# A ring of exponentials with 21 instead of 14 tiles, and a smaller reserve for GpSimd's DMA descriptors

## The chip, the cores and the metric

The kernel runs on one core of a Trainium2 chip. The engines of the core work side by side, each through its own list of instructions in order: TensorE (PE in the profile; its weight loads are shown as PEld), VectorE (DVE), ScalarE (ACT), GpSimd (POOL) and SyncE (SP), whose queue issues the DMAs. They wait for each other through semaphores. The metric is device time in microseconds (us) from one execution of the program; several runs are made and the median is given.

## The reference

One transformer block on 2048 rows of 512 numbers: layer norm, attention with 32 query heads of width 16 that share one key and one value head, and a gate from a dense Mish layer.

```python
def _A_ref(x, wq, wk, wv, wo):
    B, S, D = x.shape
    H = 32
    Dh = D // H
    q = (lambda x, *d: x.transpose(*d))((x @ wq).reshape(B, S, H, Dh), 0, 2, 1, 3)
    k = x @ wk
    v = x @ wv
    scores = jnp.einsum("bhqd,bkd->bhqk", q, k) * (Dh ** -0.5)
    p = _softmax(scores, axis=-1)
    o = jnp.einsum("bhqk,bkd->bhqd", p, v)
    return (lambda x, *d: x.transpose(*d))(o, 0, 2, 1, 3).reshape(B, S, H * Dh) @ wo
...
x = A_x
xn = _layernorm(x, axis=-1)
s = _A_ref(xn, A_wq, A_wk, A_wv, A_wo)
g = _silu(_B_ref(xn, B_w1, B_b1, B_w2))
return x + s * g
```

`_B_ref` is a dense layer 512 to 1792, Mish, and a dense layer back to 512. Everything is float32.

## The kernel before, in words

The queries are cut into 4 chunks of 512 rows, and each chunk's 32 heads into 8 groups of 4 heads. That gives 32 groups `v`, and each group runs over the 16 blocks of 128 keys: 512 **steps** `s`. After a start of some 85 us, in which x is loaded, normalised and transposed and keys and values are made, a loop over the steps writes out the order of every engine by hand. In one step stand:

- four score matmuls `e` (line 908, function `e_one`): 128 keys against 512 queries of one head. A head takes 64 of TensorE's 128 rows, so two matmuls on different halves of the rows run at once. Their results go to a pool of three PSUM banks (`ps_e`), in turn. The fourth score of a step therefore takes the bank that the first one of the same step had, after ScalarE has read it.
- four exponentials `pt` on ScalarE (line 910), one for each score, 128 x 512, written to SBUF tiles of 2 KiB a partition with the tag `pt`. These tiles are **the ring**: `NPT` of them, used in turn. The step's exponentials are named `pt{s}_0` to `pt{s}_3`.
- about four matmuls `m` (line 928, `m_one`), scores of a later group, whose row maxima VectorE takes (`mb`, line 932). The maxima go back into the query tiles `qt` through DMAs, so that the exponential gets shifted scores.
- four to nine matmuls `xps` (line 112) of the projections and of the dense layers, as two half matmuls each. The function `waves` deals these, `e` and `m` out to the two halves of the rows. Between the two halves of a projection chunk it adds a wait by hand ("other half of the bank"): the first matmul of the second half waits for an operation of the step before, in most steps the third exponential.
- at the step's end four matmuls `pv` (line 982; eight rows in the profile), which multiply the exponentials of an earlier step by the values. `pv_to(s - 2)` puts them two steps behind, so a tile is read by the end of the third step after it was written. In the last 20 steps the order is another: there are no `m`, up to six scores stand in a row, and `pv` of several steps are done together.

Beside the four exponentials ScalarE has at most one or two other operations a step (Mish and the normalisation, as exponentials and logarithms: lines 671 to 763 and 1006 to 1010).

A tile that is used again brings waits with it. The exponential that writes a ring slot must wait until `pv` has read the slot's old content, and until the old exponential has written it; the first is a wait on PE's semaphore, which the exponential has anyway for its score, and the second is one on ScalarE's own semaphore (`Activation`). Where other waits make sure of it already, the wait is left out when the program is built. An instruction holds one wait; for a second one, a separate wait instruction is put ahead of it in the engine's list (EVENT_SEMAPHORE in the trace).

At the start the ring's tiles also take the 16 blocks of x (`load_x`):

```python
tag, n = ("pt", NPT) if 4 * c + tt < NPT else (("y0", "sc")[tt % 2], 1)
...
pt = sb.tile([P, C], F32, tag="pt", name=f"pt{s}_{i}", bufs=NPT)
r = act.activation(pt, e, AF.Exp, scale=0.25)
```

The first line above is line 215, the last two are 909 and 910. All DMAs are issued from SyncE's queue. The program also holds a reserve in SBUF for the descriptors of DMAs that GpSimd would issue, 16 KiB a partition at address 0 unless asked for otherwise.

Of the kernel before, what the change touches and what calls it, by code (L numbers as in the profile page):

```python
# [42 lines left out]
HOLD = 1  # L43
STEP_US = 2.95
XMAX = 8
NPT = 14
EM = "MEMEMEME"
MLAG = 4
NHB = 4
# [69 lines left out]
def block_kernel(ctx: ExitStack, tc: tile.TileContext, x, wq, wk, wv, wo, w1, b1, w2, out):  # L119
# [93 lines left out]
    def load_x(c):  # L213
        for tt in range(4):
            tag, n = ("pt", NPT) if 4 * c + tt < NPT else (("y0", "sc")[tt % 2], 1)
            xin[c, tt] = sb.tile([P, D], F32, tag=tag, name=f"xin{c}_{tt}", bufs=n)
# [680 lines left out]
    def e_one(s, i):  # L897
# [10 lines left out]
        pe.matmul(e, ks[o:o + 64, P * k:P * (k + 1)], q[o:o + 64, p], start=True, stop=True)  # L908
        pt = sb.tile([P, C], F32, tag="pt", name=f"pt{s}_{i}", bufs=NPT)
        r = act.activation(pt, e, AF.Exp, scale=0.25)  # L910
# [487 lines left out]

# [10 lines left out]
```

## Time and profile before

| | us |
|---|---|
| median of 3 runs | 1607.55 |
| lowest, highest | 1606.56, 1608.75 |
| span of the profiled execution | 1607.2 |
| TensorE busy | 1590.6 |
| VectorE busy | 1344.9 |
| ScalarE busy | 1298.3 |
| GpSimd busy | 625.4 |

The profile is of one execution. Of it the span is given, from the first to the last instruction; no other time of its own is listed. A line such as L910 names the line of the kernel that issued an instruction. "Busy" means that an instruction of the engine was under way; a matmul that waits inside the engine counts as busy. In lists of waits the row "ACT pt L910 <- PE e L908: 240.9, 455, 1.4" reads: ScalarE's exponentials sat idle until a score matmul for 240.9 us in total, 455 times, 1.4 us at the longest. Timeline rows are start, length, engine, line, operation, output <- inputs, count of merged instructions, and in brackets the idle time before and what ended it. Engine names with a q (ACTq) are what the engine's instruction queue does by itself.

### The profile page before, as it was taken

How to read it: one execution, taken by the hardware profiler on the slowest of the kernel's cores; microseconds unless marked ns; L12 is line 12 of the kernel's file. 1: busy time of each engine (PE TensorE's matmuls, PEld its weight loads, DVE VectorE, ACT ScalarE, POOL GpSimd, SP SyncE). 2: the span in 40 equal slices, each digit the busy share in tenths (PEclk: the TensorE clock that was granted, in tenths of full speed). 3: DMA queues.
4: the chain of work that ended last, by engine and by line, in shares of the span. 5: the costliest groups of instructions: out<-in, count | busy, mean ns of one | idle time of the engine just before them, and what ended most of it. 6: DMA issues, size and time to landing. Idle time of an engine off the chain costs nothing.

```text
span 1607.2 us, 31497 instructions
## 1 busy us (share of the span) xinstructions
PE 1590.6 (99%) x11611; PEld 847.8 (53%) x11611; DVE 1344.9 (84%) x2299; ACT 1298.3 (81%) x2512; POOL 625.4 (39%) x640
## 2 busy tenths in 40 slices
PE   9999999999999999999999999999999999999998
PEld 5445555555555555555555555555555555555544
DVE  8898888888888888888898988888888888888812
ACT  7478788688898778978988787787798878779885
POOL 3276278066355103612514322172152323315522
PEclk9899999999999999999999999999999999999999
DMA  6233133142321304212103231221331223022020
GB/s 192 72 116 96 51 108 115 29 149 83 101 90 38 111 16 140 64 48 88 39 24 109 64 116 44 87 71 35 96 109 58 83 61 97 24 96 70 8 86 27
DMA packets 73001, 125.08 MB, mean 78 GB/s; under 512 B 21520, under 2 KB 33808, under 8 KB 72848
## 3 DMA queue, kind: packets, MB, share of 16 engines
q1 hardware_dynamic: 72848, 123.08, 24.4%
q8 instruction: 92, 1.51, 0.4%
q14 instruction: 61, 0.50, 0.1%
HBM read 75.57 MB, written 26.21 MB: 63 GB/s over the span
## 4 chain that ended last, share of the span: by engine, by line
PE 96%; DVE 1%; ACT 1%; POOL 0%; DMA 0%; SPq 0%; issue 0%; DVEq 0%; POOLq 0%
PE xps L112 43%; PE pv L982 32%; PE e L908 9%; PE m L928 8%; PE xps L108 3%; PE kp L312 1%; DVE mb L932 1%; PE wop L108 1%; ACT pt L910 0%; PE xp L280 0%; DMA xin<-in_dram 0%; DVE xt L156 0%; SPq L217 0%; ACT hb L671 0%; PE ol L1045 0%
## 5 line engine op out<-in xcount | busy, mean ns | idle before, releaser
L932 DVE TENSOR_REDUCE mb<-m 128x1 f32<-128x512 f32 x2048 | 1271.2, 682 | 184.2 <-PE m L928 149.0
L910 ACT ACTIVATE pt<-e 128x512 f32<-128x512 f32 x2048 | 1068.2, 605 | 250.9 <-PE e L908 240.9
L928 PE MATMUL m<-ks,qt 48*128 48x512 f32 (+1 forms) x2048 | 845.8, 424 | 4.2 <-DVE mb L932 2.9
L908 PE MATMUL e<-qt,ks 64*128 64x512 f32 x2048 | 746.7, 408 | 2.4 <-ACT pt L910 1.6
L982 PE MATMUL pv<-pt,vaug 128*32 128x512 f32 x4096 | 543.1, 604 | 0.0
L928 PEld LDWEIGHTS m<-ks,qt 48*128 48x128 f32 (+1 forms) x2048 | 373.1, 186 | 76.3 <-DVE mb L932 38.0
L908 PEld LDWEIGHTS e<-qt,ks 64*128 64x128 f32 x2048 | 372.4, 186 | 26.2 <-ACT pt L910 11.1
L112 PE MATMUL xps<-xt,ws 64*128 64x512 f32 x1266 | 351.2, 409 | 0.9 <-ACT pt L910 0.4
L112 PEld LDWEIGHTS xps<-xt,ws 64*128 64x128 f32 x1266 | 218.0, 185 | 204.8 <-ACT pt L910 137.7
L112 PE MATMUL xps<-wbs,act 64*128 64x512 f32 x1188 | 321.3, 407 | 0.0
L112 PEld LDWEIGHTS xps<-wbs,act 64*128 64x128 f32 x1188 | 207.0, 185 | 168.7 <-ACT pt L910 103.9
L166 POOL TENSOR_SCALAR t<-t 128x512 f32<-128x512 f32 x56 | 34.4, 614 | 323.8 <-ACT t L679 323.8
L982 PEld LDWEIGHTS pv<-pt,vaug 128*32 128x32 f32 x4096 | 81.9, 108 | 144.1 <-issue 135.8
L156 POOL TENSOR_TENSOR hb<-hb,t 128x512 f32<-128x512 f32 x56 | 72.2, 1289 | 116.1 <-ACT t L692 64.1
L112 PE MATMUL xps<-xt,wq 64*128 64x512 f32 x336 | 93.0, 409 | 0.0
L112 PEld LDWEIGHTS xps<-xt,wq 64*128 64x128 f32 x336 | 57.9, 185 | 54.1 <-ACT pt L910 35.2
L112 PE MATMUL xps<-wbs,ot_all 64*128 64x512 f32 x288 | 79.4, 408 | 0.0
L112 PEld LDWEIGHTS xps<-wbs,ot_all 64*128 64x128 f32 x288 | 49.5, 184 | 46.9 <-ACT pt L910 31.0
L156 POOL TENSOR_TENSOR hb<-hb,u 128x512 f32<-128x512 f32 x56 | 72.2, 1290 | 4.4
L156 POOL TENSOR_TENSOR u<-u,t 128x512 f32<-128x512 f32 x56 | 71.8, 1281 | 4.7
L156 POOL TENSOR_TENSOR act<-hb,act 128x512 fp32r<-128x512 f32 x55 | 70.7, 1286 | 4.6
L156 POOL TENSOR_TENSOR oc<-oc,sc 128x512 f32<-128x512 f32 (+1 forms) x16 | 20.6, 1287 | 121.3 <-ACT sc L1010 110.6
(121 smaller groups left out, 822.4 us busy)
## 6 DMA issues: line engine op xcount, KB each, us to landing
ws<-w SPq DMA_DIRECT2D x38, 512.0 KB
wbs<-w SPq DMA_DIRECT2D x36, 512.0 KB
qt<-qh SPq DMA_DIRECT2D x256, 32.0 KB
wq<-wq SPq DMA_DIRECT2D x14, 512.0 KB
w<-wbs SPq DMA_DIRECT2D x14, 512.0 KB
w<-ws SPq DMA_DIRECT2D x14, 512.0 KB
wbs<-wo SPq DMA_DIRECT2D x12, 512.0 KB
rawwb<-in_dram SPq DMA_DIRECT2D x20, 256.0 KB
```

The lines of the kernel that those rows point to most:

```text
L108: self.pe.matmul(ps, self.lhs(), self.rhs(), start=(self.k == 0), stop=(self.k == self.tot - 1))
L112: i = self.pe.matmul(ps, self.lhs()[o], self.rhs()[o], start=(self.k == 0 and self.halves == 0), stop=(self.k == self.tot - 1 and self.hal ...
L156: eng.tensor_tensor(out=o, in0=a, in1=b, op=op)
L166: pool.tensor_scalar(o, o, lim, 0.0, op0=ALU.min, op1=ALU.max)
L312: pe.matmul(kp_of[c], wkf[:, dt], xf_of[c][dt // 2][:, dt % 2], start=(dt == 0), stop=(dt == 3))
L908: pe.matmul(e, ks[o:o + 64, P * k:P * (k + 1)], q[o:o + 64, p], start=True, stop=True)
L910: r = act.activation(pt, e, AF.Exp, scale=0.25)
L928: pe.matmul(m, q[o, p, P * t:P * (t + 1)], ks[o, C * kb:C * (kb + 1)], start=True, stop=True)
L932: return dve.reduce_max(out=mb_of[v][:, kb, z:z + 1], in_=m, axis=AX.X)
L982: pe.matmul(o[32 * j:32 * j + 32], vaug[:, k], pt, start=(k == 0), stop=(k == 15))
```

## The change

The ring gets 21 tiles. They need 7 x 2 = 14 KiB a partition more, and 15 KiB of them come from GpSimd's descriptor reserve, which shrinks to 1 KiB. Since the ring has 21 tiles, all 16 blocks of x lie in it at the start; before, blocks 14 and 15 lay in two other tiles (`y0` and `sc`). Nearly every tile of SBUF lies at another address than before.

```diff
@@ -43,7 +43,7 @@
 HOLD = 1
 STEP_US = 2.95
 XMAX = 8
-NPT = 14
+NPT = 21
 EM = "MEMEMEME"
 MLAG = 4
 NHB = 4
@@ -1398,7 +1398,8 @@

 def kernel(A_x, A_wq, A_wk, A_wv, A_wo, B_x, B_w1, B_b1, B_w2):
     arrays = [np.asarray(a) for a in (A_x, A_wq, A_wk, A_wv, A_wo, B_w1, B_b1, B_w2)]
-    nc = bacc.Bacc("TRN2", target_bir_lowering=False, num_devices=1)
+    nc = bacc.Bacc("TRN2", target_bir_lowering=False, num_devices=1,
+                   dynamic_dma_scratch_size=1024)
```

The instructions stand in the same order on every engine. The waits are the same on TensorE, VectorE, GpSimd and SyncE, in kind and in count. On ScalarE they differ, since a slot now comes round after 21 exponentials: 14 is 3 steps and 2 tiles, so before, a step's first exponential takes the slot of a third one (and the third that of a first one); 21 is 5 steps and 1 tile, so the second takes the slot of a first one.

ScalarE in steps 233 and 234 (in the middle of the loop), before. A name is the tile, the step and the place in the step; in brackets stand the semaphores that the instruction waits for:

```order
L910 ACTIVATE pt233_0_11283<-e233_0_11281 128x512 [waits PE_49]
L910 ACTIVATE pt233_1_11292<-e233_1_11290 128x512 [waits PE_49]
L910 ACTIVATE pt233_2_11301<-e233_2_11299 128x512 [waits PE_49]
L910 ACTIVATE pt233_3_11308<-e233_3_11306 128x512 [waits PE_49]
L688 ACTIVATE t1_13_11135<-u1_13_11136,two_86 128x512 [waits Pool_49]
L910 ACTIVATE pt234_0_11322<-e234_0_11320 128x512 [waits PE_49,Activation_49]
L910 ACTIVATE pt234_1_11331<-e234_1_11329 128x512 [waits PE_49]
```

The same place in the change:

```order
 L910 ACTIVATE pt233_3_11308<-e233_3_11306 128x512 [waits PE_49]
 L688 ACTIVATE t1_13_11135<-u1_13_11136,two_86 128x512 [waits Pool_49]
-L910 ACTIVATE pt234_0_11322<-e234_0_11320 128x512 [waits PE_49,Activation_49]
+L910 ACTIVATE pt234_0_11322<-e234_0_11320 128x512 [waits PE_49]
 L910 ACTIVATE pt234_1_11331<-e234_1_11329 128x512 [waits PE_49]
```

The first exponential of step 234 has lost its wait on ScalarE's own semaphore, and with it the separate wait instruction.

ScalarE in steps 29 and 30, early in the loop:

```order
-L910 ACTIVATE pt29_0_2207<-e29_0_2205 128x512 [waits PE_49,Activation_49]
-L910 ACTIVATE pt29_1_2216<-e29_1_2214 128x512 [waits PE_49]
+L910 ACTIVATE pt29_0_2207<-e29_0_2205 128x512 [waits PE_49]
+L910 ACTIVATE pt29_1_2216<-e29_1_2214 128x512 [waits PE_49,Activation_49]
 L910 ACTIVATE pt29_2_2225<-e29_2_2223 128x512 [waits PE_49]
 L910 ACTIVATE pt29_3_2232<-e29_3_2230 128x512 [waits PE_49]
-L910 ACTIVATE pt30_0_2257<-e30_0_2255 128x512 [waits PE_49,Activation_49]
-L910 ACTIVATE pt30_1_2266<-e30_1_2264 128x512 [waits PE_49]
+L910 ACTIVATE pt30_0_2257<-e30_0_2255 128x512 [waits PE_49]
+L910 ACTIVATE pt30_1_2266<-e30_1_2264 128x512 [waits PE_49,Activation_49]
```

Here the second wait moves from the first exponential of the step to the second one. All these waits on ScalarE's own semaphore are for exponentials that lie 10 or more ScalarE operations back. In the whole program 316 exponentials have two waits before (236 first, 1 second, 77 third and 2 fourth ones of a step) and 136 in the change (1 first, 134 second, 1 fourth). Six other ScalarE operations of the last chunk get a wait on ScalarE's own semaphore that they did not have; one of them gets a separate wait instruction by it.

TensorE in step 234, the same before and in the change (`e234_3` takes the bank of `e234_0` and waits for its exponential):

```order
L908 MATMUL e234_0_11320<-qt2_79,ks_98 128x512
L112 MATMUL xps_11275<-xt2_9025,ws29_11095 128x512
L928 MATMUL m15_1_28_11325<-ks_98,qt0_77 128x512 [waits DVE_49]
L112 MATMUL xps_11275<-xt2_9025,ws29_11095 128x512
L908 MATMUL e234_1_11329<-qt2_79,ks_98 128x512
L112 MATMUL xps_11275<-xt2_9025,ws29_11095 128x512
L928 MATMUL m15_1_29_11334<-ks_98,qt0_77 128x512 [waits DVE_49]
L112 MATMUL xps_11275<-xt2_9025,ws29_11095 128x512
L908 MATMUL e234_2_11338<-qt2_79,ks_98 128x512 [waits Activation_49]
L928 MATMUL m15_0_29_11342<-ks_98,qt0_77 128x512 [waits DVE_49]
L908 MATMUL e234_3_11345<-qt2_79,ks_98 128x512 [waits Activation_49]
L982 MATMUL pv14_11009<-pt233_0_11283,vaug_100 32x512
```

Nothing moved there. In the four exponentials of the last 20 steps that wait for a `pv` which stands behind their own score in TensorE's order (`pt493_2`, `pt493_3`, `pt499_2`, `pt499_3`), the wait is for an earlier point of TensorE's list: the slot they take was last read 21 exponentials back.

## The prediction

> **What bounds the kernel now.** I read the page first, then the waits, then two neighbouring steps of the main loop in the timeline, then four stretches of equal work.
>
> ```profile
> span 1607.2 us, 31497 instructions
> PE 1590.6 (99%) x11611; PEld 847.8 (53%) x11611; DVE 1344.9 (84%) x2299; ACT 1298.3 (81%) x2512; POOL 625.4 (39%) x640
> PE 96%; DVE 1%; ACT 1%; POOL 0%; DMA 0%; SPq 0%; issue 0%; DVEq 0%; POOLq 0%
> q1 hardware_dynamic: 72848, 123.08, 24.4%
> ```
>
> By this page TensorE is the bound and nothing that ScalarE waits for can matter. That reading is too coarse: a matmul that has been let into the array and stands there for a bank counts as busy. Next, what the exponentials (line 910) wait for, and what that line issues:
>
> ```profile
> ACT pt L910 <- PE e L908: 240.9, 455, 1.4
> ACT pt L910 <- PE pv L982: 1.6, 2, 0.8
> L910 ACT ACTIVATE pt<-e x2048: 584/601/690, 85.5 to 1586.2; 128x512 f32<-128x512 f32 x187
> L910 ACTq EVENT_SEMAPHORE  x316: 17/17/17, 125.7 to 1578.6; - x158
> ```
>
> Two facts. The ring itself is hardly ever the wait: of 2048 exponentials two waited for `pv`, the reader that frees a slot, 1.6 us together. And 316 exponentials carry a second instruction, a separate wait on ScalarE's own queue, because they wait for two semaphores. It lasts 17 ns in its row. What it costs is seen in two steps that follow each other: step 233 has none, step 234 has one ahead of its first exponential. Columns: start, length, engine, line, operation.
>
> ```profile
> 770.92 0.39 PE L908 MATMUL e<-qt,ks 64*128 64x512 f32 x1
> ...
> 771.35 2.06 ACT L910 ACTIVATE pt<-e 128x512 f32<-128x512 f32 x4 [0.21 <-PE e L908]
> ...
> 771.39 0.39 PE L908 MATMUL e<-qt,ks 64*128 64x512 f32 x1
> ...
> 772.09 0.41 PE L908 MATMUL e<-qt,ks 64*128 64x512 f32 x1
> ...
> 772.43 1.06 PE L982 MATMUL pv<-pt,vaug 128*32 128x512 f32 x8
> ...
> 773.42 0.18 PEld L112 LDWEIGHTS xps<-xt,ws 64*128 64x128 f32 x1 [0.84 <-ACT pt L910]
> ...
> 773.77 0.39 PE L908 MATMUL e<-qt,ks 64*128 64x512 f32 x1
> ...
> 774.26 2.06 ACT L910 ACTIVATE pt<-e 128x512 f32<-128x512 f32 x4 [0.23 <-PE e L908]
> ...
> 774.93 0.47 PE L908 MATMUL e<-qt,ks 64*128 64x512 f32 x1
> ...
> 775.34 1.06 PE L982 MATMUL pv<-pt,vaug 128*32 128x512 f32 x8
> ...
> 776.67 0.40 PE L908 MATMUL e<-qt,ks 64*128 64x512 f32 x1
> ```
>
> Step 233: the first score matmul at 770.92, its exponential 0.43 us later, the last score at 772.09, `pv` at 772.43, the next step at 773.77: 2.85 us. Step 234: the first exponential comes 0.49 us after its score, 0.06 later; the last score is in the array for 0.47 instead of 0.41 us; `pv` starts 0.41 instead of 0.34 us after it; the step takes 2.90. The code says why. Scores have three PSUM banks, so a step's fourth score reuses the bank of its first and must wait for the first exponential's end. It does so **inside** TensorE's busy time. The four exponentials then run without gaps (2.06 us for four in both steps), so only the first one's start counts.
>
> Four stretches, each cut at the first score of a step, with the score matmuls alone; the exponentials of the first carry no extra waits, those of the second 7 in 7 steps, all on first exponentials:
>
> ```profile
> 1463.26:1483.19 19.93, 10.01 (x28) 5.20 (x28) 1.00 0.24 73
> 915.06:935.49 20.43, 10.49 (x28) 5.21 (x28) 1.00 0.09 28
> 1368.14:1386.45 18.31, 8.98 (x24) 4.47 (x24) 1.00 0.13 39
> 983.49:1007.96 24.47, 12.22 (x32) 5.96 (x32) 1.00 0.30 93
> ```
>
> ```profile
> L910 ACTq EVENT_SEMAPHORE  x7: 17/17/17, 915.5 to 933.0; - x7
> L910 ACTq EVENT_SEMAPHORE  x14: 17/17/17, 983.9 to 1006.3; - x14
> ```
>
> The columns of the first four rows are the stretch, its length, the busy time of those matmuls and of their weight loads, clock, DMA share, GB/s. The first two stretches are 7 steps each: 19.93 / 7 = 2.847 and 20.43 / 7 = 2.919 us. The difference, 0.50 us, stands almost whole in the scores' own busy time (10.49 - 10.01 = 0.48): **0.07 us for each step that has the extra wait**. The last two are 6 and 8 steps, in which one more piece of projection work lies between the third and the fourth score: 18.31 / 6 = 3.052 without and 24.47 / 8 = 3.059 with the extra wait on each first exponential (8 of its 14; the other 6 stand on third exponentials). There it costs nothing, because the fourth score comes late enough.
>
> **The change, part by part.** No engine's order of work changes, and only ScalarE's waits do.
>
> *Extra waits that go.* In the order of before, 236 of the 316 stand on a step's first exponential, 77 on the third, 3 elsewhere; in the order of the change it is 1 on the first, 134 on the second, 1 on the fourth. So 235 first exponentials lose theirs. For 234 of those (steps 10 to 489) I counted how long after TensorE's last `e` or `m` matmul the `pv` starts. It falls into two heaps: 163 steps at 0.35 us or more, middle 0.404 (the `pv` of the first and of the last of them, steps 14 and 485, stand below); 71 steps at 0.32, as in the fourth stretch, with nothing between the heaps. The 246 steps without it have their middle at 0.346.
>
> ```profile
> 126.88 1.06 PE L982 MATMUL pv<-pt,vaug 128*32 128x512 f32 x8
> 1511.45 1.07 PE L982 MATMUL pv<-pt,vaug 128*32 128x512 f32 x8
> ```
>
> So the price is 0.404 - 0.346 = 0.058 us in 163 steps and nothing in 71: 163 x 0.058 = **9.5 us**. The ends: 71 ns each by the stretches gives 11.6; 60 ns in all 236 gives 14.2. I take 9.5, since it comes from the most steps and agrees with the pair above. The 77 on third exponentials are worth nothing: those stand in a queue behind the second (four run in 2.06 us either way).
>
> *Extra waits that come.* 134 second exponentials get one. Without it they start when the first is through, 0.49 us after its start; their own score comes 0.47 us after the first (771.39 against 770.92), so 0.02 us of a delay of 0.06 is covered and they are at most 0.04 us late. Behind them on ScalarE stand the third and fourth exponentials. Who waits for those: the second half of a projection chunk, for the third exponential, and scores of the next step, for the second to fourth. In step 233 the third exponential ends about 0.43 + 2.06 - 0.48 = 2.01 us after the first score and the projection starts at 773.42, 2.50 us after it. So 0.04 disappears in 0.49 us of slack. I take 0; the ends are 0 and 134 x 0.04 x 163/234 = 3.7 us lost.
>
> *The deeper ring.* The two waits for `pv` stand near the end, in steps 493 and 499; the second:
>
> ```profile
> 1551.14 1.09 ACT L910 ACTIVATE pt<-e 128x512 f32<-128x512 f32 x2 [0.83 <-PE pv L982]
> 1553.30 3.04 ACT L910 ACTIVATE pt<-e 128x512 f32<-128x512 f32 x6 [1.07 <-PE e L908]
> ```
>
> Both go, since a slot 21 back has been read long before. But the exponentials behind it wait for the next scores anyway, 1.07 us, and TensorE is then still at a run of `pv`; 0.83 us earlier on ScalarE only makes that 1.9. Value 0, ends 0 and 1.6 us gained. Why the others never bind: `pv` of a slot's last use stands ahead of the next score in TensorE's own order.
>
> *The first loads and the reserve.* Two tiles of x move from borrowed buffers into the ring, with no other wait; GpSimd issues no DMA (all 123 MB go through the hardware queue of the page), so its reserve is used by nothing. Both 0. Addresses of nearly all tiles shift; see the third rival.
>
> *What is late next.* Step 233's stretch shows it: steps of 2.847 us run seven in a row, so neither VectorE nor DMA holds them above that. One DMA wait of TensorE in the loop can grow a little when steps get shorter:
>
> ```profile
> PE e L908 <- DMA qt<-cr: 0.8, 1, 0.8
> ```
>
> Within the 16 steps of one such transfer 0.06 x 16 = 1 us is the most it could take back.
>
> **Sum.** 1607.2 - 9.5 = 1597.7 us for the profiled execution's span. No other time of that execution is given; its span lies 0.35 us under the median of the three runs (1607.55; 1606.56 to 1608.75), and with that 1598.0.
>
> The Trainium skill speaks against this term: "VectorE: DVE Perf Modes", section "The DRAIN you can't avoid", reports a chain of VectorE copies equally long with a semaphore after each and with one alone, so that the semaphore costs nothing extra. By it the sum would be 1607.5, as in rival 1. The rows agree with it where ScalarE has a queue (four exponentials in 2.06 us either way) and not where ScalarE stands idle for the score (0.43 against 0.49 us).
>
> **The rivals.**
>
> 1. *No change* (within 0.2%, that is 3.2 us, about what a measurement of this kernel can tell from none). The extra wait would only be a mark of steps that are longer for another reason, and the deeper ring gives at most its 1.6 us: 1606 to 1607.5. For it: TensorE 99% busy. Against it: the 0.06 us appears between score and exponential, again at the fourth score and again at `pv`, and is missing where the fourth score is late. 0.08.
>
> 2. *Smaller gain.* What holds the step is ScalarE's chain as a whole, so the 134 second exponentials pay 3.7 us, and DMA takes back 1: 1598.0 + 4.7 = 1602.7. Against it: the 0.49 us of slack above. 0.12.
>
> 3. *Slower.* The shifted addresses make ScalarE's exponential longer, in the place that holds the short steps: the first one's end frees the bank. By the same count 362 steps are of that kind (163 with and 199 without the extra wait), so each 10 ns costs 3.6 us; the gain is gone at 26 ns, and it is slower by 0.2% from 35 ns on, an exponential of 636 instead of 601 ns. At 45 ns: 1598 + 16 = 1614. For it: the row's own spread, 584 to 690. Against it: the ring's 14 slots lie at 14 addresses already, and half of the exponentials still lie between 584 and 601. 0.03. The Trainium skill, "SBUF — State Buffer", section "Who interferes with whom", says that TensorE and ScalarE wait for no other engine's access; by that this rival falls away, and no run here shows it yet.
>
> **How the numbers follow.** The forecast, 1593 to 1601.5, has 0.77; rival 2 has 0.12, rival 1 0.08, rival 3 0.03. The low end, 1593, is 14.2 us under 1607.2; the high end, 1603, takes in rival 2. Faster by over 0.2% (under 1604.3): 0.77 + 0.12 = 0.89. Same: 0.08. Slower: 0.03.
>
> **What would show it.** In the changed kernel's profile: the separate waits of line 910 fall from 316 to 136; the distance from the first score to its exponential is 0.43 us in nearly all steps; the score matmuls' busy time over the program falls by about 9 us; stretches with second exponentials that carry the wait run at 2.85 us a step; no exponential waits for `pv`. Wrong would be: `pv` still 0.40 us behind the fourth score, now held by something else; steps with the wait on the second exponential at 2.9 us; or a longer middle of the exponential's row.

## The result and the profile after

| | before | after |
|---|---|---|
| median | 1607.05 us (4 runs, 1604.81 to 1608.75) | 1599.16 us (4 runs, 1598.17 to 1602.02) |
| ratio | | 0.995, 95% interval 0.9937 to 0.9963 |
| span of the profiled execution | 1607.2 us | 1597.8 us |
| TensorE, VectorE, ScalarE busy | 1590.6, 1344.9, 1298.3 us | 1580.7, 1344.8, 1303.4 us |

The kernel is 0.5% faster. First the page of the changed kernel: the span, the engines, and the group of the score matmuls; the last line is the same group on the page before.

```profile
span 1597.8 us, 31318 instructions
PE 1580.7 (99%) x11611; PEld 838.2 (52%) x11611; DVE 1344.8 (84%) x2299; ACT 1303.4 (82%) x2512; POOL 625.4 (39%) x640
PE 96%; DVE 2%; ACT 1%; DMA 0%; POOL 0%; issue 0%; SPq 0%; DVEq 0%; POOLq 0%
...
L908 PE MATMUL e<-qt,ks 64*128 64x512 f32 x2048 | 736.0, 402 | 2.4 <-ACT pt L910 1.6
...
L908 PE MATMUL e<-qt,ks 64*128 64x512 f32 x2048 | 746.7, 408 | 2.4 <-ACT pt L910 1.6
```

TensorE is as "full" as before, 99%, and its matmuls are the same in number. Yet it was busy for 9.9 us less. The scores alone fell from 746.7 to 736.0 us: time that had been counted as work was waiting inside the matmul. The profile models the ends of matmuls, so the lengths alone would be weak evidence; the starts of `pv` and of the next step, below, moved by about as much.

What line 910 issues on ScalarE in the changed kernel (count, shortest, middle and longest length in ns, first and last start in us):

```profile
L910 ACT ACTIVATE pt<-e x2048: 589/600/692, 84.5 to 1576.7; 128x512 f32<-128x512 f32 x187
L910 ACTq EVENT_SEMAPHORE  x136: 17/17/17, 169.8 to 1543.9; - x136
```

The separate waits fell from 316 to 136. From the first to the last exponential it is 1576.7 - 84.5 = 1492.2 us, where it was 1586.2 - 85.5 = 1500.7 before: 8.5 us by these rounded times, 8.4 by the unrounded ones of the traces. The rest of the 9.4 us between the two spans lies ahead of the first exponential (84.5 against 85.5), where nothing was expected; the experiments below show that this part differs from one execution to the next.

Step 233, step 234 and the first score of step 235 in the timeline of the changed kernel:

```profile
766.22 0.39 PE L908 MATMUL e<-qt,ks 64*128 64x512 f32 x1
766.65 2.06 ACT L910 ACTIVATE pt<-e 128x512 f32<-128x512 f32 x4 [0.20 <-PE e L908]
...
769.08 0.39 PE L908 MATMUL e<-qt,ks 64*128 64x512 f32 x1
769.51 2.06 ACT L910 ACTIVATE pt<-e 128x512 f32<-128x512 f32 x4 [0.18 <-PE e L908]
...
770.25 0.40 PE L908 MATMUL e<-qt,ks 64*128 64x512 f32 x1
770.58 1.07 PE L982 MATMUL pv<-pt,vaug 128*32 128x512 f32 x8
...
771.91 0.40 PE L908 MATMUL e<-qt,ks 64*128 64x512 f32 x1
```

Step 234 now looks like step 233 did. Its first exponential comes 0.43 us after the score (0.49 before), its fourth score takes 0.40 us (0.47), `pv` follows 0.33 us later (0.41), and the step takes 2.83 us (2.90).

Where the 0.06 us had come from is seen in the separate wait's own row, here that of step 234 in the kernel before:

```profile
L910 ACTq EVENT_SEMAPHORE  x1: 17/17/17, 774.2 to 774.2; - x1
```

It starts 0.43 us after the step's first score (773.77), which is when the exponential itself starts in a step without it; the exponential starts at 774.26. By the operands in the trace, the separate instruction is the one that waits for the score (TensorE's semaphore), and the exponential itself holds the wait that has long been satisfied (ScalarE's own semaphore). So the late wait stands in the separate instruction. In the 234 steps of 10 to 489 that have it, this instruction starts 0.433 us after the score and the exponential 0.062 us after the instruction (middles); without it, in the changed kernel, a first exponential that ScalarE stood idle for starts 0.435 us after its score.

The first two stretches of the prediction, cut again at the same steps (469 to 475, and 283 to 289), with the score matmuls alone:

```profile
1453.89:1473.85 19.96, 10.02 (x28) 5.20 (x28) 1.00 0.26 73
909.58:929.74 20.16, 10.22 (x28) 5.20 (x28) 1.00 0.09 28
```

The stretch without separate waits stayed (19.93 to 19.96 us). The one with them fell from 20.43 to 20.16, which is 0.27 us where seven times 0.07 would be 0.49. Steps 283 to 285 did reach 2.85 us; step 286 shows what came late next. Its matmuls and VectorE's work, in the changed kernel:

```profile
918.50 0.21 DVE L961 STREAM_TRANSPOSE cr<-mp 128x32 f32<-128x32 f32 x1 [0.21 <-DVE mp L956]
...
918.64 2.44 DVE L932 TENSOR_REDUCE mb<-m 128x1 f32<-128x512 f32 x4
...
919.34 0.49 PE L928 MATMUL m<-ks,qt 48*128 48x512 f32 x1
919.35 0.49 PE L908 MATMUL e<-qt,ks 64*128 64x512 f32 x1
919.77 1.07 PE L982 MATMUL pv<-pt,vaug 128*32 128x512 f32 x8
```

VectorE has just put a group's maxima in order (the transpose at 918.50) and so begins its four reductions 0.84 us after the step's first `m` (917.80), where it takes 0.56 us in each of the three steps before. The step's fourth `m` takes the bank of the first and waits for VectorE: it takes 0.49 us, as does the fourth score beside it. Step 286 takes 2.97 us, more than before (2.92). In such steps VectorE took the place of ScalarE.

The two waits of exponentials for `pv` near the end are gone. What stands in place of the second, in the changed kernel (the view ends at 1545 us and cuts the second row off there; it goes on to six exponentials):

```profile
1537.84 4.02 ACT L910 ACTIVATE pt<-e 128x512 f32<-128x512 f32 x8
1543.87 1.58 ACT L910 ACTIVATE pt<-e 128x512 f32<-128x512 f32 x3 [2.01 <-PE e L908]
```

Eight exponentials run in one piece, and then ScalarE waits 2.01 us for the next scores, where it waited 0.83 for `pv` and 1.07 for the scores before. Nothing is gained by it: the part of the time from the first to the last exponential that lies outside steps 10 to 489 is 89.9 us in both traces.

Counted over steps 10 to 489 of the two traces (one pair of executions): the 163 steps that the prediction counted as held are 8.95 us shorter in all, 55 ns each; the 71 that it counted as not held are longer by 0.07 us in all; the 246 that had no separate wait on the first exponential are longer by 0.51 us in all, 2 ns each. Of the 163, there are 149 in which the fourth score's row still ends 0.55 us after the end of the first exponential, as in the kernel before: these still wait for the first exponential, which now comes earlier, and are 9.37 us shorter. In the other 14 the fourth `m` was held by VectorE as in step 286, and they are longer by 0.42 us in all.

### The profile page after: what moved, and what is told of

Same layout as the page of the kernel before. It is cut to its first block, busy times and chain, and to the rows that moved or that the text cites. A ratio compares the mean times of both kernels' runs of the same rounds, so it can differ in the third digit from the quotient of the medians.

```text
span 1597.8 us, 31318 instructions
## 1 busy us (share of the span) xinstructions
PE 1580.7 (99%) x11611; PEld 838.2 (52%) x11611; DVE 1344.8 (84%) x2299; ACT 1303.4 (82%) x2512; POOL 625.4 (39%) x640
## 4 chain that ended last, share of the span: by engine, by line
PE 96%; DVE 2%; ACT 1%; DMA 0%; POOL 0%; issue 0%; SPq 0%; DVEq 0%; POOLq 0%
PE xps L112 44%; PE pv L982 32%; PE m L928 8%; PE e L908 8%; PE xps L108 3%; DVE mb L932 1%; PE kp L312 1%; PE wop L108 1%; ACT pt L910 0%; PE xp L280 0%; DMA xin<-in_dram 0%; DVE xt L156 0%; ACT hb L671 0%; PE ol L1045 0%; DMA qt<-cr 0%
## 5 line engine op out<-in xcount | busy, mean ns | idle before, releaser
L908 PE MATMUL e<-qt,ks 64*128 64x512 f32 x2048 | 736.0, 402 | 2.4 <-ACT pt L910 1.6
L982 PEld LDWEIGHTS pv<-pt,vaug 128*32 128x32 f32 x4096 | 81.8, 108 | 144.3 <-issue 136.1
```

Of the source, the lines that this page charges most:

```text
L982: pe.matmul(o[32 * j:32 * j + 32], vaug[:, k], pt, start=(k == 0), stop=(k == 15))
```

## The experiments

Theory A: the separate wait ahead of a step's first exponential is what costs, through the fourth score that waits for this exponential. Theory B: the depth of the ring gives the gain. Theory C: the smaller reserve, or the new addresses, give it. The best measure is the time from the first to the last exponential, from the row of their line, since the part ahead of it varies. It is 1500.7 us before and 1492.2 us after (differences below are of such rounded times, and so good to 0.1 us).

**One tile more instead of seven, and the reserve left alone.**

```diff
-NPT = 14
+NPT = 15
```

> One tile more than before (15) and GpSimd's reserve left at 16 KiB. Theory A (the separate wait ahead of a step's first exponential is what costs): in the order of this kernel 1 first exponential has it instead of 236, and 193 second ones, so nearly the whole gain: span 1598 to 1599 us, 8 to 9 us under before. Theory B (the depth of the ring gives the gain): one seventh of it, 1606. Theory C (the smaller reserve or the new addresses): nothing, 1607.

1599.53 us, ratio 0.9947 (0.9931 to 0.9963). The row of line 910:

```profile
L910 ACT ACTIVATE pt<-e x2048: 587/599/682, 82.4 to 1574.6; 128x512 f32<-128x512 f32 x187
L910 ACTq EVENT_SEMAPHORE  x198: 17/17/17, 123.0 to 1567.1; - x198
```

1574.6 - 82.4 = 1492.2 us, the same as with 21 tiles. One tile and no other reserve give the whole gain, although 198 separate waits are left; 193 of them stand on second exponentials. Theory C falls by this, and so does theory B as a gain that grows with each tile. That 15 tiles might just be deep enough is not excluded by this run, but by the next. The counting fits: with an odd number of tiles a step's first exponential never takes the slot of a first or third one, and in all four rings that were built (14, 15, 20 and 21 tiles) nearly all the second waits stand on exponentials that do. Why the build can leave the wait out for the slots of second and fourth ones was not looked into.

**A ring of 20 tiles**, six more than before, with the small reserve.

```diff
-NPT = 21
+NPT = 20
```

> Ring of 20 tiles with the reserve of 1 KiB. 20 is a whole number of steps, and 168 first exponentials have the separate wait, 110 of them in steps where the fourth score waits for the first exponential. Theory A: 110 x 0.058 = 6.4 us of the gain are lost again: span near 1604. Theory B: 6 of 7 more tiles, so 1599. Theory C: 1598.

1604.67 us, ratio 0.9977 (0.9963 to 0.9991).

```profile
L910 ACT ACTIVATE pt<-e x2048: 588/602/692, 89.5 to 1587.2; 128x512 f32<-128x512 f32 x187
L910 ACTq EVENT_SEMAPHORE  x216: 17/17/17, 132.5 to 1554.3; - x108
```

1587.2 - 89.5 = 1497.7 us: 5.5 us of the 8.5 are lost again, where theory A had said 6.4. A ring of 20 is slower than one of 15, so it is not the depth.

**The reserve alone.**

```diff
-    nc = bacc.Bacc("TRN2", target_bir_lowering=False, num_devices=1)
+    nc = bacc.Bacc("TRN2", target_bir_lowering=False, num_devices=1,
+                   dynamic_dma_scratch_size=1024)
```

> Ring of 14 tiles as before, only the reserve shrunk to 1 KiB, so that nearly all addresses shift. Theory A and B: no change from before, span 1607 within 1.5 us. Theory C: the gain is there, 1598.

1608.05 us, ratio 0.9996 (0.9984 to 1.0007): no change.

```profile
L910 ACT ACTIVATE pt<-e x2048: 588/601/692, 90.4 to 1590.9; 128x512 f32<-128x512 f32 x187
L910 ACTq EVENT_SEMAPHORE  x316: 17/17/17, 130.6 to 1583.4; - x158
```

1590.9 - 90.4 = 1500.5 us against 1500.7, with nearly every tile at another address. Step by step, the 480 steps differ by 0.1 us in all from those of before.

**The separate wait put back, ahead of every first exponential.** The changed kernel with, in `e_one` behind the exponential:

```diff
+        if i == 0 and s < NS - LEAD and 3 in last_pt:
+            tc.add_manual_dep(r.ins, last_pt[3].ins.name, mybir.DependencyInfo(
+                mybir.DependencyClass.Sync, mybir.DependencyReason.DATA), reason="second wait")
+        last_pt[i] = r
```

> The changed kernel (21 tiles, 1 KiB), with a wait added by hand to the first exponential of each step up to step 491, for the last exponential of the step before, which is long done; this makes the separate wait stand ahead of all those 492 first exponentials. Theory A: 0.058 us in each of the 352 steps whose fourth score waits for the first exponential, 20 us: span near 1618, slower than before. Theories B and C: 17 ns a wait at most, and ScalarE is idle 19% of the time, so 1598.

1617.78 us, ratio 1.0057 (1.0044 to 1.0071): slower than before, with the deep ring and the small reserve. Its rows (one line was added above, so the exponential has line 911 here and the score 909), and the two stretches of steps 469 to 475 and 283 to 289:

```profile
L911 ACT ACTIVATE pt<-e x2048: 587/602/684, 83.7 to 1594.9; 128x512 f32<-128x512 f32 x187
L911 ACTq EVENT_SEMAPHORE  x493: 17/17/17, 86.8 to 1562.1; - x165
...
L909 PE MATMUL e<-qt,ks 64*128 64x512 f32 x2048 | 758.0, 413 | 2.4 <-ACT pt L911 1.6 <-DMA qt<-cr 0.8
```

```profile
1471.05:1491.42 20.37, 10.46 (x28) 5.20 (x28) 1.00 0.22 73
919.65:940.09 20.44, 10.52 (x29) 5.20 (x28) 1.00 0.08 27
```

1594.9 - 83.7 = 1511.2 us, 19.0 more than the changed kernel, for 20 expected. The stretch that ran without separate waits in both kernels now has them, and takes 20.37 instead of 19.96 us: 0.059 us a step. The scores' busy time is 758.0 us. This is the causal test: the added wait is for an exponential that is done (in 476 of the 480 steps at least 0.19 us before the separate instruction passes, in the middle 0.79 us), so it holds nothing by what it waits for. It holds by making the score's wait pass through a separate instruction: in this trace too that instruction waits for TensorE's semaphore, and the exponential starts 0.062 us behind it.

**The same wait ahead of every second exponential** (`i == 1` in the same edit).

> The changed kernel with the same added wait on the second exponential of each step up to step 491 instead of the first: 492 separate waits on second exponentials, none on first ones. Theory A (only the first exponential's end is waited for, by the fourth score): nothing, first to last exponential 1492 us as in the changed kernel, span near 1598. Rival (the chain of four exponentials as a whole holds the step): 0.04 us in some 350 steps beyond those 134 that have it, 10 to 14 us, span near 1609.

1598.79 us, ratio 0.9944 (0.9923 to 0.9964).

```profile
L911 ACT ACTIVATE pt<-e x2048: 587/599/682, 87.4 to 1579.8; 128x512 f32<-128x512 f32 x187
L911 ACTq EVENT_SEMAPHORE  x493: 17/17/17, 90.9 to 1546.9; - x165
```

1579.8 - 87.4 = 1492.4 us. As many separate waits as in the last kernel, one place further on, cost 0.2 us instead of 19.0. The delay itself is there. The four exponentials of a step in this kernel:

```profile
775.25 2.10 ACT L911 ACTIVATE pt<-e 128x512 f32<-128x512 f32 x4 [0.23 <-PE e L909]
```

They take 2.10 us instead of 2.06, since the second one starts 0.527 us after the first instead of 0.495 (middles over steps 10 to 489). The step is not longer by it. So it is not the number of waits on ScalarE, and not its chain of four exponentials.

**The first score earlier.** If the fourth score waits too long for the first exponential, one could start the first score earlier.

```diff
-EM = "MEMEMEME"
+EM = "EMMEMEME"
```

> The changed kernel with the first score of a step one place earlier among TensorE's score and maximum matmuls, ahead of the first m, which comes one place (0.23 us) later. Theory A: the first exponential ends 0.2 us earlier for the fourth score, which no longer waits: up to 0.03 us in 352 steps, 10 us, span near 1588, if nothing else takes its place. What could: the fourth m takes the bank of the first m, whose maximum now comes 0.23 us later against a slack of some 0.1 us; then 0.1 us a step is lost, and the span is 1610 to 1635.

1650.48 us, ratio 1.0264 (1.0235 to 1.0293). It went the second way, and further: the time lies above the 1610 to 1635 us expected for it. Steps 10 to 489 are 51 us longer in all, the middle step by 0.12 us, 415 of the 480 by more than 0.05. One step of it, TensorE's last two score and maximum matmuls and VectorE:

```profile
793.24 2.48 DVE L932 TENSOR_REDUCE mb<-m 128x1 f32<-128x512 f32 x4 [0.49 <-PE m L928]
...
793.99 0.50 PE L928 MATMUL m<-ks,qt 48*128 48x512 f32 x1
793.99 0.51 PE L908 MATMUL e<-qt,ks 64*128 64x512 f32 x1
794.43 1.06 PE L982 MATMUL pv<-pt,vaug 128*32 128x512 f32 x8
```

```profile
PEld m L928 <- DVE mb L932: 130.8, 383, 0.8
...
PEld m L928 <- DVE mb L932: 25.9, 69, 0.8
```

The fourth `m` and the score beside it stand for 0.50 us, and in the loop (78 to 1570 us) the loads of `m` wait for VectorE's maxima 383 times, 130.8 us in all; the second row is the changed kernel's (78 to 1530 us): 69 times, 25.9 us. An `m` that came 0.23 us later cost 0.12 us a step, so in the order of before VectorE's banks had only some 0.1 us to spare (an estimate from these two numbers), and this version is no improvement.

**The early first score with the wait ahead of every first exponential.** Both edits together.

> The kernel with the early first score, with the added wait on all first exponentials as well. Theory A: the early place gives the first exponential over 0.2 us of room, so the wait of 0.06 us costs nothing there: within 2 us of the kernel with the early first score alone, where the same wait cost 18 us in the order of before. Rival (a wait ahead of an idle ScalarE costs wherever it stands): 18 to 28 us more than the early first score alone.

1648.81 us, ratio 1.026 (1.0229 to 1.0291), and from the first to the last exponential 1544.0 us:

```profile
L911 ACT ACTIVATE pt<-e x2048: 589/598/682, 81.8 to 1625.8; 128x512 f32<-128x512 f32 x187
L911 ACTq EVENT_SEMAPHORE  x493: 17/17/17, 84.9 to 1592.9; - x165
```

The kernel with the early first score alone has 1544.0 us as well (86.0 to 1630.0). The same 492 waits on the same exponentials that cost 19.0 us in the old order cost nothing here, since now something else is late. The delay is there all the same: the first exponential starts 0.60 us after its score instead of 0.54 (middles), but the second starts no later than without it. That excludes a price for a separate wait as such.

## Why the prediction was right

*The bound.* The step that carried it, that a busy TensorE hides a wait for a PSUM bank inside the last score matmul, is shown: the scores' busy time moves with the waits (736.0 us after, 746.7 before, 758.0 with all of them), while the count of matmuls and their idle time stay. The fourth score's row ends 0.55 us after the first exponential's end (middle) in all three kernels.

*The extra waits that go.* 9.5 us were forecast, 163 steps at 0.058 us. These steps gave 8.95 us, 55 ns each, and the loop as a whole 8.4. The mechanism and the place were right. The part ahead of the prediction speaks of the separate instruction as the second, long satisfied wait, and the prediction does not say why that should delay anything; the trace shows that it holds the wait for the score. The term was a little too large, because it let every step fall to the bound of the others. In 149 of the 163 steps it did (9.37 us, 63 ns each); in 14 VectorE held the step, as in step 286, and nothing was gained. "Neither VectorE nor DMA holds them" was read from one stretch of seven steps, with 29 operations on VectorE where the other stretch had 33.

*The extra waits that come.* Valued at 0, with 3.7 us as the bad end, since the second exponential would be at most 0.04 us late and slack would take it. It was 0.03 us late, and with 492 instead of 134 such waits the loop took 0.2 us more: 0 is right, and rival 2 falls.

*The deeper ring* was worth nothing, as forecast: 15 tiles do as much as 21. *The reserve and the addresses* were worth nothing: 0.9996, interval 0.9984 to 1.0007. So rival 3 falls; the exponential's middle was 601 ns before and 600 after.

*No change*, rival 1, had held that the wait is only a mark of longer steps. Putting the wait into steps that had been short made them longer by 0.059 us. It falls. The sentence of the Trainium skill in "VectorE: DVE Perf Modes" ("The DRAIN you can't avoid") that a semaphore costs nothing extra is measured on a chain of VectorE copies, and for separate waits on ScalarE the runs differ from it. The first exponentials were 0.06 us late by theirs and the second ones 0.03; only where the exponential stood further back in the queue was nothing lost (in the 54 steps of the kernel before with one on the first and one on the third exponential, the third starts 477 ns after the second, as it does without).

*The sum.* The span was forecast at 1597.7 and came at 1597.8. That closeness is partly luck: the loop gave some 1 us less than the 9.5, and the start, which had no term, gave some 1 us. The median was forecast at 1598.0 and came at 1599.16, in the range. Of that difference the offset from span to time is a part: 0.35 us had been taken, while the profiled execution after has 1599.6 us for a span of 1597.8, which is 1.8. By the medians the gain is 7.9 us. The prediction names two high ends, 1601.5 and 1603; the result lies under both.

*The signs.* Those of being right came, except that the first exponential starts 0.43 us after its score in fewer steps than "nearly all": less than 0.45 us after it in 368 of the 480 steps, against 174 before. Steps that carry the wait on the second exponential take 2.87 us in the changed kernel (middle) and 2.86 in the kernel that has it in all steps, against 2.86 without.

What stays open: a separate wait lasts 17 ns in its row, and the exponential starts 62 ns after the row's start. The traces do not show where the other 45 ns go. No kernel had the two waits the other way round, with the satisfied one in the separate instruction and the score's on the exponential; whether the delay would then vanish is not shown. Nor was it tried to take the last 0.03 us out of the short steps by giving scores a fourth bank: the program's four PSUM pools already take 3 + 3 + 1 + 1 buffers.

## What to carry to other kernels

When an engine is 99% busy, compare the length of one and the same instruction between steps: here a matmul that took 0.47 instead of 0.41 us held a wait, and the wait's cause was on another engine. Before a ring is made deeper, look whether anything waits for it; here it hardly ever did (two waits, 1.6 us in all), and what helped was that its size became odd against a step of four. Look at the waits that a build adds, also those that are long satisfied: each second wait can bring an instruction of its own, and here it cost where ScalarE stood idle and its next result was waited for. Look, too, at which of the two waits the separate instruction holds: here it was the late one.

## What the runs showed of the hardware

That TensorE's clock differs from one execution to the next in the first 80 us was not expected. Its granted value there and the first exponential's start, in the executions that were profiled (the stretch 0 to 80 us: length, busy time of TensorE; the clock stands ahead of the last two columns), of the kernel with 15 tiles, the kernel before, and the one with the reserve alone:

```profile
0.00:80.00 80.00, 75.22 (x282) 41.56 (x282) 70.36 (x147) 45.69 (x103) 29.54 (x40) 0.96 0.42 133
...
0.00:80.00 80.00, 74.20 (x270) 41.14 (x271) 68.34 (x141) 45.55 (x102) 26.39 (x37) 0.91 0.41 133
...
0.00:80.00 80.00, 74.37 (x261) 40.90 (x262) 66.78 (x136) 43.09 (x98) 24.79 (x35) 0.89 0.42 133
```

With 0.96 the first exponential starts at 82.4 us, with 0.91 at 85.5, with 0.89 at 90.4; from 80 to 1500 us the clock is 1.00 in all of them. Over all nine profiled executions the clock goes from 0.88 to 0.98 and the start from 90.4 to 81.8 us; the two go together, though not strictly (another execution with 0.89 starts at 87.4), and no run shows that the clock alone makes the start. The kernel before ran between 1603.52 and 1614.16 us in its 35 runs, which is 10.6 us, and the first exponential's start differed by 8.6 us over the profiled executions, while the loop behind it agreed within 0.2 us between kernels whose first exponentials carry the same waits (1492.2, 1492.2, 1492.4 and 1500.7, 1500.5). So for a change in the loop the time from the first to the last exponential of a single execution says more than the median of several whole times.
